# A fused attention and soft mixture-of-experts kernel: a list scheduler for the whole program, one pool of PSUM banks, and filler matmuls on TensorE

## The chip, the cores and the metric

One core of one Trainium2 chip runs the kernel. The metric is the device time of one execution in microseconds (us), lower is better. Executions of this kernel differ by some per cent: the kernel before gave 249 to 264 us. How long the chip grants TensorE its full clock differs from run to run (mean granted clock 0.68 to 0.79 before; the mean counts the time before the first recorded change as full). A run is called fast when it is within 1.5% of the fastest of its kernel, and slow otherwise. I quote medians of all runs, and the fast runs or their ratio where they say something else. Kernels ran beside runs of the kernel before.

## The reference

Eight batches of eight heads of windowed attention feed a soft mixture of experts. Cut to what matters:

```python
B, H, S, D = 8, 8, 576, 64                    # q, k, v: float32
scores = q @ k.T / 8                          # per batch and head
mask   = (rel >= 0) & (rel < 32)              # heads 0..3
       | (rel >= 0) & (rel < 128) & (rel % 4 == 0)   # heads 4..7
x = softmax(scores where mask) @ v            # -> (4608, 512)
logits = x @ phi                              # (4608, 32): 8 experts, 4 slots each
slot_in  = softmax(logits, over tokens).T @ x
slot_out = relu(slot_in[e] @ w1[e]) @ w2[e]   # w1 512x1024, w2 1024x512
out = softmax(logits, over slots) @ slot_out
```

## The kernel before

A batch is worked in two groups of four heads, so there are 16 groups g. In the loop TensorE does, for each group: `st_A` 72 staging transposes of q, k, v (four blocks of 18), `st_B` transposes of V, `st_S` scores (four blocks of 6), `st_P` probabilities times V (two blocks of 12), and for each batch `st_X` transposes of the result, `st_L` logits (8 dense matmuls of 288 columns), `st_E` and `st_I`, 48 narrow matmuls of 32 columns that accumulate into the PSUM bank `psA`. ScalarE evacuates st_A and does the exponentials; VectorE does the masks and the rest. The order of everything is written by hand, and PSUM banks come from two rings:

```python
ps2 = [... [128, 2, 512] ... for i in range(2)]     # two-bank tiles, two of them
ps1 = [... [128, 512] ...    for i in range(3)]     # one-bank tiles, three of them
psA = ...                                           # the accumulator
...
for step in range(-1, 2 * B + 2):
    if on: st_B(g, 0); st_S(g, 0, 0)
    if nx: st_A(g + 1, 0)
    if on: st_S(g, 0, 1)
    if nx: st_A(g + 1, 1)
    if pr: st_P(g - 1, 1)
    ...
    if odd: st_I(b - 1); st_X(b, 0); st_X(b, 1)
# loads, GpSimd queue: w1[0], q/k/v of batch 0 (whole), w1[1], q/k/v of batch 1, ...
```

After the loop come the two expert layers (`ffn1`, `ffn2`) and the output, 18 tiles.

The softmax here doesn't subtract the row's maximum and nothing guards it: scores larger than these inputs give would overflow.

## Time and profile before

| | before |
|---|---|
| median of the runs beside the change | 258.65 us (254.61 to 261.89, 4 runs) |
| profiled span | 261.6 us |
| first transposes start | 17.77 us |
| first expert matmul starts | 218.11 us |
| from there to the end | 43.5 us |

The page of the kernel before: span, busy time of TensorE (PE), VectorE (DVE), ScalarE (ACT), then in 40 slices of 6.5 us the busy tenths of TensorE, the granted clock in tenths, and the DMA engines' share.

```profile
span 261.6 us, 7056 instructions
PE 209.8 (80%) x3055; PEld 160.1 (61%) x3056; DVE 121.1 (46%) x237; ACT 125.2 (48%) x302; POOL 30.6 (12%) x68
PE   0027998999899989989998999899888758888700
PEclk9999999997557555555575575555555555999955
DMA  6999999999999509998910664178037700007998
```

TensorE is 90% busy or more through most of the loop, and the others aren't. The clock row reads half speed over most of it. Its first nine digits can't be taken at their word: the record holds changes of the clock, and reads full before the first one. The timeline of TensorE shows this (columns: start us, length us, engine, line, operation, tiles, shape, count).

```profile
27.03 0.93 PE L307 MATMUL ps_2<-ident,stg 96*64 96x96 bf16 x18
...
55.44 2.12 PE L417 MATMUL ps_0<-XT,phi_pad 128*128 128x288 bf16 x8
...
59.81 0.57 PE L307 MATMUL ps_2<-ident,stg 96*64 96x96 bf16 x18
60.31 0.73 PE L377 MATMUL ps_1<-VN,PT 128*96 128x65 bf16 x12
60.97 1.63 PE L457 MATMUL psA<-ET,XB 96*64 96x32 bf16 x48
62.53 0.66 PE L398 MATMUL ps_0<-ident,XB 96*128 96x96 bf16 x6
```

Eighteen staging transposes took 0.93 us at 27 us, where the clock row still says full, and 0.57 us at 59.81 us, so the loop was slow from its start. It got its full clock for one short stretch (58.4 to 61.8 us) after the dense logit matmuls of L417, and fell back. Four such stretches, 13.7 us, are all of the loop's 200.3 us: **7% at full clock**. That is the low end: this was a slow run, with a mean granted clock of 0.69, where the fast runs of this kernel had 0.75 to 0.79. No trace of those was kept. I work out this share the same way for every kernel below: stretches of full clock between the first transposes and the first expert matmul, leaving out the time before the first change where the transposes are slow.

The windows view of two batches (columns: busy us of PE, PEld, DVE, ACT and POOL with counts, granted clock, DMA share, GB/s), then the longest TensorE wait from the waits view:

```profile
84.40:109.20 24.80, 23.73 (x360) 19.48 (x358) 13.59 (x26) 14.87 (x38) 3.24 (x6) 0.53 0.66 129
109.20:132.60 23.40, 22.22 (x357) 18.18 (x357) 12.70 (x25) 12.91 (x34) 1.65 (x3) 0.55 0.95 191
...
PE ps_0 L307 <- DMA stg<-in_v_dram: 17.8, 1, 17.8
```

A batch takes 23.4 to 24.8 us, 95% of it TensorE busy at little more than half clock (0.53 and 0.55). Nothing waits long but the start.

### The profile page before, as it was taken

The page shows a single profiled execution, that of the slowest core. Times are in us where ns is not written, and L with a number is a line of the kernel's source. Part 1 is how long each engine was busy: PE and PEld are TensorE (multiplying, and loading weights), DVE is VectorE, ACT ScalarE, POOL GpSimd, SP SyncE. Part 2 cuts the span into 40 slices and gives each one's busy share as a digit, 9 for nine tenths or more (in the row PEclk, how much of TensorE's full clock was granted, in tenths as well). Part 3 has the DMA queues.
Part 4 walks back from the last instruction along what each step waited for, and adds up shares of the span by engine and source line. Part 5 has one row for each costly group of instructions (what it writes and reads, how often), then busy time and mean ns, then how long its engine had stood idle before and what let it go on. Part 6 is the DMA issues. An engine that isn't in the chain of part 4 may idle for free.

```text
span 261.6 us, 7056 instructions
## 1 busy us (share of the span) xinstructions
PE 209.8 (80%) x3055; PEld 160.1 (61%) x3056; DVE 121.1 (46%) x237; ACT 125.2 (48%) x302; POOL 30.6 (12%) x68
## 2 busy tenths in 40 slices
PE   0027998999899989989998999899888758888700
PEld 0025787778787867877787878778766734531100
DVE  0001557636644565466366545644664521219900
ACT  1017785565576545645655764456463010008900
POOL 7970300300030022002000000000000000000000
PEclk9999999997557555555575575555555555999955
DMA  6999999999999509998910664178037700007998
GB/s 110 207 219 208 220 209 217 214 215 212 219 198 216 118 4 189 220 219 153 215 37 3 114 113 99 19 148 147 18 38 137 152 0 3 3 0 289 406 404 345
DMA packets 8910, 40.88 MB, mean 156 GB/s; under 512 B 1456, under 2 KB 1456, under 8 KB 6832
## 3 DMA queue, kind: packets, MB, share of 16 engines
q0 software_dynamic: 5760, 30.94, 60.4%
q1 hardware_dynamic: 3120, 9.50, 9.2%
q8 instruction: 24, 0.39, 0.6%
q14 instruction: 6, 0.05, 0.0%
HBM read 61.93 MB, written 9.44 MB: 273 GB/s over the span
## 4 chain that ended last, share of the span: by engine, by line
PE 60%; ACT 10%; DMA 10%; DVE 9%; issue 4%; POOL 2%; POOLq 0%; ACTq 0%
DMA stg<-in_v_dram 10%; PE ps_1 L377 5%; PE psA L457 5%; PE ps_0 L377 4%; PE ps_2 L307 4%; PE ps_0 L307 4%; PE ps_1 L307 3%; PE ps_1 L587 3%; PE ps_0 L352 3%; PE ps_1 L417 3%; PE ps_0 L417 3%; DVE XB L386 3%; DVE w1r L612 3%; PE ps_1 L352 3%; ACT PT L358 3%
## 5 line engine op out<-in xcount | busy, mean ns | idle before, releaser
L307 PE MATMUL ps_0<-ident,stg 96*64 96x96 bf16 x414 | 21.2, 280 | 17.8 <-DMA stg<-in_v_dram 17.8
L358 ACT ACTIVATE PT<-ps_0 128x576 bf16<-128x576 f32 x32 | 21.1, 660 | 26.8 <-PE ps_0 L352 26.7
L358 ACT ACTIVATE PT<-ps_1 128x576 bf16<-128x576 f32 x32 | 21.1, 660 | 25.3 <-PE ps_1 L352 25.3
L361 DVE TENSOR_TENSOR PT<-PT,mask_d 128x576 bf16<-128x576 bf16 x32 | 14.7, 458 | 37.4 <-ACT PT L358 37.4
L307 PEld LDWEIGHTS ps_0<-ident,stg 96*64 96x64 bf16 x414 | 17.0, 162 | 20.7 <-POOL siT L293 17.7
L361 DVE TENSOR_TENSOR PT<-PT,mask_p 128x576 bf16<-128x576 bf16 x32 | 14.7, 458 | 25.8 <-ACT PT L358 25.1
L307 PE MATMUL ps_2<-ident,stg 96*64 96x96 bf16 x396 | 19.8, 275 | 0.2 <-DMA stg<-in_v_dram 0.2
L318 ACT ACTIVATE QT<-ps_0 128x288 bf16<-128x288 bf16 x23 | 10.4, 451 | 18.6 <-PE ps_0 L307 18.6
L377 PE MATMUL ps_1<-VN,PT 128*96 128x65 bf16 x192 | 17.8, 262 | 0.4 <-ACT PT L358 0.4
L377 PE MATMUL ps_0<-VN,PT 128*96 128x65 bf16 x192 | 17.8, 263 | 0.0
L307 PEld LDWEIGHTS ps_2<-ident,stg 96*64 96x64 bf16 x396 | 15.9, 159 | 3.1 <-issue 0.3
L377 PEld LDWEIGHTS ps_1<-VN,PT 128*96 128x96 bf16 x192 | 15.7, 183 | 2.3 <-PE ps_0 L352 0.6
L307 PE MATMUL ps_1<-ident,stg 96*64 96x96 bf16 x342 | 17.0, 274 | 0.0
L337 DVE COPY VN<-ps_1 128x768 bf16<-128x768 bf16 x12 | 6.6, 548 | 22.1 <-PE ps_1 L333 22.1
L377 PEld LDWEIGHTS ps_0<-VN,PT 128*96 128x96 bf16 x192 | 15.8, 184 | 1.6
L386 DVE TENSOR_TENSOR XB<-ps_0,RV 96x768 bf16<-96x768 f32 x16 | 15.3, 954 | 0.6
L386 DVE TENSOR_TENSOR XB<-ps_1,RV 96x768 bf16<-96x768 f32 x16 | 15.3, 953 | 0.6
L226 POOL DMA_DIRECT2D stg<-in_q_dram x8 | 4.4, 553 | 93.1 <-PE ps_1 L307 39.5
L307 PEld LDWEIGHTS ps_1<-ident,stg 96*64 96x64 bf16 x342 | 13.6, 158 | 2.4
L457 PE MATMUL psA<-ET,XB 96*64 96x32 bf16 x384 | 13.0, 217 | 0.6 <-DVE ET L443 0.6
L352 PE MATMUL ps_0<-QT,KT 64*128 64x96 bf16 x192 | 13.3, 267 | 0.0
L352 PE MATMUL ps_1<-QT,KT 64*128 64x96 bf16 x192 | 13.3, 267 | 0.0
(114 smaller groups left out, 377.8 us busy)
## 6 DMA issues: line engine op xcount, KB each, us to landing
out_dram<-w1r SPq DMA_DIRECT2D x18, 512.0 KB, 5.1
w1r<-in_moe_w_dram POOLq DMA_DIRECT2D x8, 1024.0 KB, 21.3
stg<-in_moe_w_dram POOLq DMA_DIRECT2D x6, 1024.0 KB, 8.0
stg<-in_q_dram POOLq DMA_DIRECT2D x8, 576.0 KB, 12.7
stg<-in_k_dram POOLq DMA_DIRECT2D x8, 576.0 KB, 14.8
stg<-in_v_dram POOLq DMA_DIRECT2D x8, 576.0 KB, 17.0
w2r<-in_moe_w_dram POOLq DMA_DIRECT2D x2, 1024.0 KB, 21.7
phi_st<-in_moe_phi_dram SPq DMA_DIRECT2D x1, 64.0 KB, 2.0
```

The source lines that it names most:

```text
L307: i_ = t.transpose(pbf[64 * hx:64 * hx + 64, NR * i:NR * i + NR], stg_x[s][0:NR, 2 * typ + hx, c, :], ident[0:NR, 0:NR])
L318: op("act", lambda ac, d=d, t=t: ac.activation(d, pv[:, t], ACTF.Copy), r=[pb], **{"w" if r == 0 else "a": [bd[par]]})
L337: op("dve", lambda vv: vv.tensor_copy(vt[:, half, :, :, 0:64], pbf[:, 0:768].rearrange("p (m x d) -> p m x d", m=NB, x=2)), r=[pb], w=[vb[ ...
L352: i_ = t.matmul(sc[:, hx, QB * mm:QB * mm + QB], KT[par][64 * hx:64 * hx + 64, half, QB * m:QB * m + 128], QT[par][64 * hx:64 * hx + 64, h ...
L358: op("act", lambda ac: ac.activation(pt[:], sc[:, :, 0:3 * QB], ACTF.Exp, scale=SCALE), r=[scb], w=[ptb])
L361: op("dve", lambda vv: vv.tensor_tensor(pt[:], pt[:], mk.unsqueeze(1).to_broadcast([128, 2, 3 * QB]), AluOp.mult), r=[b_mask[typ]], w=[ptb])
L377: i_ = t.matmul(po[0:QB, hx, 65 * m:65 * m + 65], pts[m // 3][0][:, hx, QB * (m % 3):QB * (m % 3) + QB], vt[:, half, m, hx, 0:65], start=T ...
L386: op("dve", lambda vv: vv.tensor_tensor(xd, pv[:, :, :, 0:64], rv[:].unsqueeze(3).to_broadcast([QB, 2, NB, 64]), AluOp.mult), r=[pob, rvb] ...
L417: i_ = t.matmul(lg[:, hf, 0:288], phi_pad[:, c].rearrange("p j i -> p (j i)"), XT[:, c, 288 * hf:288 * hf + 288], start=c == 0, stop=c == 3)
L457: i_ = t.matmul(psA[64 * typ:64 * typ + 64, 32 * c:32 * c + 32], x_, et[:, NB * typ + m, :], start=(b == 0 and m == 0 and c == 0), stop=(b ...
L587: i_ = t.matmul(sp_[32 * j:32 * j + 32, :], hT[:, hi, cc, j, :], w2v[e][:, cc, :], start=(hi == 0 and cc == 0), stop=(hi == 1 and cc == 7))
L612: op("dve", lambda vv, o=o, po=po: vv.tensor_scalar(ost[:, o % NO, 1, :], po[:, 1, :], rtok[:, 2 * o + 1:2 * o + 2], None, op0=AluOp.mult) ...
```

## The change

Its intent: let a program order the work so that TensorE never waits, and keep its clock up where it still does.

1. Work is first collected as tasks with estimated durations (taken at full clock) and due times, then placed by a list scheduler, which also picks PSUM banks from one pool of seven. The outcome is a fixed order for each engine; nothing is decided on the chip.
2. Where the plan leaves TensorE idle for 0.27 us or more, up to six unused 384-column matmuls go into spare columns of `psA` (84 in all).
3. q, k, v are loaded in halves per group, ahead of w1, and the set-up memsets moved from GpSimd to VectorE.

```diff
-    for step in range(-1, 2 * B + 2):      # hand-written order
+def place(tasks, banks, filler):
+    ...                                    # per engine: earliest start, given preds, banks
+            if e == "pe" and t.mode != last_mode[0]:
+                st += 0.13
+            m = min(c[0] for c in cands)
+            st, t = min((c for c in cands if c[0] <= m + 0.14), key=lambda c: (c[1].due, c[1].idx))
+    ...
+        if t.eng == "pe":
+            idle = st - free.get("pe", 0.0)
+            if filler is not None and order:
+                f = filler(idle, st)
...
-    ps2 = [A(nc.psum_tensor(f"ps2_{i}", [128, 2, 512], F32)) for i in range(2)]
-    ps1 = [A(nc.psum_tensor(f"ps1_{i}", [128, 512], F32)) for i in range(3)]
+    NBK = 7
+    psum = A(nc.psum_tensor("psum", [128, NBK, 512], F32))
...
-    def load_qkv(b):                       # whole batch; w1[0] before batch 0
+    def load_qkv(b, due):
+        for typ in range(2):
+            for t, src in enumerate((q, k, v)):
+                load(...)                  # half a batch each; w1[0] after batch 0
...
+    def filler(idle, st):
+        n_ = min(int((idle - 0.1) / 0.17), 6)
+        if n_ < 1 or acc_last[0].end is not None:
+            return None
+        ...
+                i_ = pe.matmul(psA[:, 128:512], ident[:, :],
+                               mask[1][:, 0:4, :].rearrange("p m x -> p (m x)"),
+                               start=False, stop=False, skip_group_check=True)
```

## The prediction

> **What bounds the kernel now.** From 17.8 us (first landing of q, k, v; before it TensorE waits 17.8 us, the longest TensorE wait) to about 209 us TensorE is 91 to 98% busy in nearly every 10 us stretch (windows view); VectorE and ScalarE are busy 45 to 65%. The chain of waits is 60% TensorE. One batch (two head groups) takes 23.75 us: the accumulation into psA starts at 61.0, 84.4, 109.2, 132.7, 156.1, 180.9, 203.5. So TensorE bounds the main loop, and it runs slowly: 18 staging transposes take 0.93 us nearly everywhere but 0.57 us in 58 to 61 and 82 to 86 us; 12 probability-times-V matmuls take 1.17 against 0.73 us. The granted clock reads 0.50 over most of 60 to 218 us. Before 57 us it reads 1.0, but the durations there are the slow ones, so I take the clock to be half there too. The fast stretches follow the eight dense 288-column logit matmuls. The Trainium skill ("TensorE: Matmul & The Clock Gate", Part 1) says the clock is halved until TensorE was busy for one window of about 3.4 us, and Part 4 that transposes don't count as busy in the same way. The trace agrees: fast stretches last about 4 us, and over half of the loop's matmuls are transposes.
>
> Loads aren't the bound: 31 MB at 215 GB/s is 144 us, and the DMA queues idle from 130 us on for want of staging buffers.
>
> **What changes.**
> 1. First landing: q, k, v come in halves and first, ahead of w1. 0.88 MB at 215 GB/s is 4 us plus issue and latency: TensorE starts near 9 us. Saves about 8 us, all on the chain.
> 2. Order: waits inside the loop are only 5% of TensorE's time; this and one bank pool give at most 1 us per batch at half clock. The end (205 to 218 us, one long dependence chain) may lose 2 us.
> 3. Filler matmuls, 384 columns each, about 0.16 us fast and 0.32 us at half clock. Alone they are cost, and TensorE has no slack at half clock. Their worth is the clock. From the fast stretches, a group needs about 6.5 us of TensorE work plus some 1.7 us of switching and waits, so about 8.2 us against 11.9 us; ScalarE needs about 6.5 and VectorE about 6 (start to start), loads 6.8 per group, so nothing else binds much earlier.
> 4. Unchanged: experts and output, 43 us from 218 us; output DMA at 405 GB/s.
>
> Always fast: 9 + 16 x 8.2 + 5 + 7 + 43 = 195 us. Always slow with fillers: 9 + 16 x 12 + 10 + 43 = 254 us. The planner places fillers only where its own (fast) plan leaves TensorE idle by 0.27 us, so they may be too thin to hold the clock everywhere. I expect fast for about three quarters of the loop: 210 us.
>
> **Predicted: 210 us, 80% between 193 and 242. Faster by over 2%: 0.93; within 2%: 0.05; slower: 0.02.**
>
> **What would show it.** Step 1: first transposes near 9 us. Step 3: granted clock near 1.0 over most of 15 to 145 us, 18 transposes near 0.57 us, batch period 16 to 18 us; TensorE busy share falls or holds while ScalarE and VectorE shares rise. Step 2: TensorE waits spread, few over 1 us. Step 4: last 43 us alike.
>
> **What would make it wrong.** The fillers are too few: clock remains 0.5, period 23 us or more, time near 250. Or the clock holds but ScalarE or the loads become the bound, with periods of 19 us. Or the last w2 tiles, whose buffers come free only after batch 7's transposes, land after the first expert layer ends.

## The result, and the profile after

The changed kernel took 209.73 us (median of 4 runs, 207.09 to 212.37), against 258.65 us. The ratio of the fast runs is 0.815, 95% interval 0.8035 to 0.8264. A ratio is the mean time of one kernel's fast runs over that of the other's of the same rounds, so it is not quite the ratio of the medians. The profiled run of the changed kernel took 211.77 us (span 210.0 us), one of its slower ones. That of before took 263.31 us, more than the four runs in the table, so the two profiles compare slow with slow.

The page of the changed kernel, the rows shown of before:

```profile
span 210.0 us, 7124 instructions
PE 169.3 (81%) x3139; PEld 125.0 (60%) x3140; DVE 119.8 (57%) x259; ACT 122.8 (58%) x302; POOL 36.1 (17%) x71
PE   0479998968999995999889998999989888798000
PEclk9999999999967998599999999557999669999955
DMA  5999999999999999999999999962990000069998
```

TensorE's busy share is nearly the same, 81% after 80%, of a shorter span: its 40 us less are the same work at a higher clock, and 84 matmuls more. The clock row is now mostly full, and here the early digits hold. The timeline of TensorE:

```profile
16.22 0.57 PE L448 MATMUL psum<-ident,stg 96*64 96x96 bf16 x18
...
128.23 0.78 PE L622 MATMUL psA<-ET,XB 96*64 96x32 bf16 x20
129.63 1.03 PE L622 MATMUL psA<-ET,XB 96*64 96x32 bf16 x28 [0.62 <-issue]
130.59 0.66 PE L553 MATMUL psum<-ident,XB 96*128 96x96 bf16 x6
131.19 0.42 PE L498 MATMUL psum<-QT,KT 64*128 64x96 bf16 x6
131.54 0.82 PE L472 MATMUL psum<-ident,VT 128*128 128x128 bf16 x6
132.29 0.93 PE L448 MATMUL psum<-ident,stg 96*64 96x96 bf16 x18
```

The clock is full from 11.1 us. It falls three times within the loop, for 6.8, 6.8 and 13.7 us; the last fall is the one above, and the transposes are back at 0.93 us. At the loop's end it falls once more. Full clock for **81% of the loop**.

Where the 51.6 us between the two profiled spans come from:

| part | before | after | gain |
|---|---|---|---|
| start to first transposes | 17.77 | 10.0 | 7.8 |
| loop, to first expert matmul | 200.3 | 156.1 | 44.2 |
| experts and output | 43.5 | 43.9 | -0.4 |

The windows view of two batches, and the two longest TensorE waits (waits view):

```profile
96.00:113.00 17.00, 15.26 (x355) 12.47 (x352) 11.93 (x25) 13.25 (x36) 1.13 (x2) 1.00 1.03 214
113.00:128.20 15.20, 14.49 (x327) 11.76 (x324) 11.80 (x25) 11.59 (x29) 1.06 (x2) 1.00 1.05 217
...
PE psA L787 <- DVE mask_d L415: 8.0, 1, 8.0
PE psum L448 <- issue: 4.3, 3, 2.1
```

These two take 17.0 and 15.2 us at full clock; the first took 19.6 us, at full clock as well. The 8.0 us are the first fillers waiting for their operand at the start, before any data is there, and "issue" is idle time for which the profile shows no cause. So the clock is the visible difference. The open question is what holds it: the fillers (theory A, the prediction's), or the planned order (theory B).

### The profile page after: what moved, and what is told of

Its sections match the earlier page's. It is cut to its first block, busy times and chain, and to the rows that moved or that the text cites. A ratio compares the mean times of both kernels' runs of the same rounds, so it can differ in the third digit from the quotient of the medians.

```text
span 210.0 us, 7124 instructions
## 1 busy us (share of the span) xinstructions
PE 169.3 (81%) x3139; PEld 125.0 (60%) x3140; DVE 119.8 (57%) x259; ACT 122.8 (58%) x302; POOL 36.1 (17%) x71
## 4 chain that ended last, share of the span: by engine, by line
PE 58%; DVE 15%; ACT 12%; issue 7%; DVEq 0%
PE psum L448 10%; PE psum L526 8%; PE psum L498 6%; PE psA L622 6%; PE psum L472 6%; DVE w1r L765 5%; PE psum L553 5%; PE psA L787 4%; PE psum L737 4%; PE psum L682 3%; PE psum L576 3%; ACT QT L458 3%; ACT PT L504 3%; ACT KT L458 2%; DVE XB L538 2%
## 5 line engine op out<-in xcount | busy, mean ns | idle before, releaser
L504 ACT ACTIVATE PT<-psum 128x576 bf16<-128x576 f32 x64 | 42.3, 668 | 28.1 <-PE psum L498 27.5
L448 PE MATMUL psum<-ident,stg 96*64 96x96 bf16 x1152 | 36.1, 225 | 4.3 <-issue 4.3
L458 ACT ACTIVATE QT<-psum 128x288 bf16<-128x288 bf16 x64 | 30.0, 468 | 12.1 <-PE psum L448 12.1
L448 PEld LDWEIGHTS psum<-ident,stg 96*64 96x64 bf16 x1152 | 31.3, 123 | 8.6 <-issue 6.5
L538 DVE TENSOR_TENSOR XB<-psum,RV 96x768 bf16<-96x768 f32 x32 | 30.5, 954 | 1.1
L458 ACT ACTIVATE VT<-psum 128x288 bf16<-128x288 bf16 x64 | 30.5, 478 | 0.4 <-PE psum L448 0.4
L458 ACT ACTIVATE KT<-psum 128x288 bf16<-128x288 bf16 x64 | 30.4, 476 | 0.0
L476 DVE COPY VN<-psum 128x768 bf16<-128x768 bf16 x32 | 17.6, 552 | 17.9 <-PE psum L472 17.9
L526 PE MATMUL psum<-VN,PT 128*96 128x65 bf16 x384 | 24.7, 217 | 2.2 <-DVE PT L507 0.8
L787 PE MATMUL psA<-mask_d,ident 128*128 128x384 bf16 x84 | 19.6, 348 | 8.0 <-DVE mask_d L415 8.0
L526 PEld LDWEIGHTS psum<-VN,PT 128*96 128x96 bf16 x384 | 21.8, 132 | 5.4 <-DVE PT L507 2.7
L498 PE MATMUL psum<-QT,KT 64*128 64x96 bf16 x384 | 20.7, 216 | 3.9 <-issue 1.5
L472 PE MATMUL psum<-ident,VT 128*128 128x128 bf16 x192 | 18.1, 237 | 0.0
```

The lines of the kernel that those rows point to most:

```text
L448: i_ = t.transpose(o[64 * hx:64 * hx + 64, NR * i:NR * i + NR], stg_x[s][0:NR, 2 * typ + hx, c, :], ident[0:NR, 0:NR])
L458: op("act", lambda ac, d=d, t=t: ac.activation(d, bf(h)[:, 0:9 * NR].rearrange("x (c t h p) -> x t h p c", c=9, t=3, h=2)[:, t], ACTF.Copy ...
L472: i_ = t.transpose(o[:, 128 * m:128 * m + 128], VT[par][:, half, QB * m:QB * m + 128], ident[:, :])
L476: op("dve", lambda vv: vv.tensor_copy(vt[:, half, :, :, 0:64], bf(h)[:, 0:768].rearrange("p (m x d) -> p m x d", m=NB, x=2)), w=[vb], ps=[ ...
L498: i_ = t.matmul(sc[:, hx, QB * mm:QB * mm + QB], KT[par][64 * hx:64 * hx + 64, half, QB * m:QB * m + 128], QT[par][64 * hx:64 * hx + 64, h ...
L504: op("act", lambda ac: ac.activation(pt[:], f32(h)[:, :, 0:3 * QB], ACTF.Exp, scale=SCALE), w=[ptb], ps=[h], dur=0.54, due=due + 0.2)
```

## The experiments

All results are correct against the reference. Times are medians, with lowest and highest.

### 1. The change without its fillers

```diff
-    for t in place(tasks, NBK, filler):
+    for t in place(tasks, NBK, None):
```

> The changed kernel with its 84 filler matmuls left out; planned order, one bank pool and loads untouched. Theory A (the fillers hold the clock, and the clock is the gain): the granted clock falls to 0.5 over most of the loop, 18 staging transposes go back to 0.93 us, time 235 to 252 us. Theory B (the planned order alone packs TensorE densely enough to hold the clock; the fillers are a cost): 200 to 210 us with the clock unchanged. In between (220 to 232): both take part.

Measured: 212.39 us (210.32 to 218.0, 4 runs), before beside it 261.14 us. The page's rows, then the windows view of one long stretch at full clock and of two batches:

```profile
PE   0279999997889899699897999987946788898000
PEclk9999999999999999859999559999955579999855
...
36.50:87.70 51.20, 44.20 (x1082) 36.99 (x1077) 36.22 (x74) 40.87 (x107) 12.84 (x24) 1.00 1.05 215
61.50:77.10 15.60, 14.14 (x341) 11.81 (x338) 12.10 (x25) 12.43 (x33) 4.32 (x9) 1.00 1.05 214
97.90:113.40 15.50, 13.51 (x345) 11.65 (x344) 11.50 (x25) 13.02 (x36) 1.13 (x2) 1.00 1.02 213
```

Theory A falls. Without any filler the loop still runs at full clock for 63% of the time, from 36.5 us on, and the kernel takes some 3 us more than the changed kernel's 209.5 us. That was on another chip; as a share of the kernel before beside each, the medians are alike (0.813 here, 0.811 and 0.817 for the changed kernel), so even these 3 us aren't sure.

The two batches of 15.5 us flatter the order. A batch is 356 matmuls of the loop's own (2848 in all, for eight), and in the planned order the time from one accumulation to the next holds more or less than that: 341 and 345 in these two, and 396 in the first, which took 18.8 us at full clock. By count, the stretch of 51.2 us makes 16.8 us a batch, and all three stretches of full clock within the loop (99.0 us, 2091 matmuls) 16.9 us. The count is a rough measure, as matmuls differ in length.

### 2 and 3. Fillers in the old order

One, and then two, of the same fillers after each of the 64 score blocks of the kernel before (psA set to zero first, as the change does):

```diff
             st_S(g, 0, 0)
+            fill(1)          # experiment 3: fill(2); likewise after the other three
```

> The kernel before, in its old order with its old banks and loads, with one 384-column filler matmul after each of the 64 score blocks. Theory A (clock is the gain): if 64 regular fillers are enough to hold the clock, about 225 us (loop period from 23.7 to about 19.5 us, start unchanged); if they are too thin they only cost 64 x 0.32 us at half clock, up to 270 us. Theory B (the order is the gain): 260 to 270 us.

> As e2 with two fillers after each score block, 128 in all. Theory A: the clock holds, 225 to 232 us, in spite of 128 more matmuls. Theory B: 270 to 285 us, the fillers being pure cost.

Measured: 247.59 us (246.85 to 258.15) with 64 fillers and 244.38 us (240.01 to 257.25) with 128, against 261.14 us. The fast runs were 246.85 to 247.59 us and 240.01 to 242.23 us, against 251.36 us, the one fast run of before; so the gain of the 64 is small. The page's clock row of the second, and a batch of it:

```profile
PEclk9999999999555799999997999999999657999955
...
106.20:126.70 20.50, 18.18 (x374) 13.28 (x372) 12.70 (x25) 13.85 (x36) 1.65 (x3) 1.00 1.04 215
```

Full clock for 55% and 76% of the loop. So dense fillers do raise the clock, and the old order gets quicker in spite of up to 128 more matmuls: neither "pure cost" nor the predicted 225 us. But 76% of full clock is close to the change's 81%, and the kernel is 35 us slower. Eight of these are the start; 128 fillers at 0.16 us are 20 us more, by estimate from the changed kernel, where six fast ones span 1.15 us with the last one's own 0.34 us ((1.15 - 0.34) / 5). The 7 us left are about what the gaps of the old order would cost (experiment 8). The old order has to buy its clock with work.

### 4 and 8. The start, from both sides

The changed kernel with w1[0] first and batch 0 waiting for both halves:

```diff
+    load_w1(0, -27.0)
     for b in range(B):
         load_qkv(b, -26.0 + b)
...
-        op("pe", pe, r=[b_id, b_in[s][typ]], ...
+        op("pe", pe, r=[b_id, b_in[s][typ]] + ([b_in[s][1]] if b == 0 else []), ...
```

> The changed kernel, but the first w1 tile is loaded ahead of q, k, v again and batch 0 waits for both its halves, so the first transposes start near 17 us instead of 10. If TensorE's own work paces the loop the 7 us come back in full: about 214 to 217 us. If something later in the loop (loads, ScalarE) sets the pace, less than 3 us: 208 to 211 us.

Measured: 216.64 us (210.71 to 218.23), first transposes at 17.84 us, loop 156.1 us as in the changed kernel. By the medians that is the seven microseconds in full, but the control ran on another chip, the profiled spans differ by 5.2 us (210.0 and 215.2, the part after the loop being 2.6 us shorter), and the one fast run, 210.71 us, is only 1.5 to 4.6 us above the control's. The loop itself took up none of the late start.

The kernel before with q, k, v in halves and ahead of w1:

```diff
-    load_w1(0)
...
     load_qkv(0)               # now two halves, each group waits for its own
-    load_w1(1)
+    load_w1(0)
```

> The kernel before with q, k, v loaded in halves per head group and ahead of w1, and nothing else of the change. If the start is worth what it moves: first transposes near 10 us, 6 to 8 us faster than before, 250 to 254 us, clock as before. If the earlier data also let TensorE hold its clock in the loop: 240 us or less. If the loop swallows it: 258 us or more.

Measured: 247.94 us (243.73 to 253.71, 6 runs) against 256.51 us; ratio of fast runs 0.9762, interval 0.9566 to 0.9959. First transposes at 9.57 us. The medians gain 8.6 us, a little above the range; the fast runs gain 6 us (2.4%), within it. So the gain is the start's. In the profiled run, a fast one, the clock was full for 27% of the loop, which gives what was missing, the old order at full clock with no fillers, in one stretch and in the batch within it:

```profile
48.20:72.10 23.90, 19.81 (x483) 16.64 (x482) 15.07 (x31) 17.74 (x46) 5.31 (x10) 1.00 1.05 213
52.20:70.40 18.20, 14.74 (x357) 12.33 (x356) 12.47 (x25) 13.38 (x36) 3.70 (x7) 1.00 1.05 213
```

By count of matmuls, all four stretches of full clock in this loop (51.2 us, 1007 matmuls) make 18.1 us a batch, against 16.9 us in the planned order of experiment 1: at the same clock, the order is worth about 1.2 us a batch. TensorE is busy 80% of the time in the first (40.90 of 51.20) and 87% in the second (86.46 of 99.00). So the planned order closes some of the gaps that the full clock opens; in the batch shown TensorE waited 2.1 us for VectorE (`XB`) and 1.2 us for ScalarE (`VT`). Loads don't pace this stretch: q, k and v of the groups begun in it had landed 9 us before or more.

### 5 and 6. The change again, and fillers at the start only

Run 5 is the changed kernel unchanged, the control. Run 6 keeps the fillers of the plan's first 36 us, 22 of 84:

```diff
-        if n_ < 1 or acc_last[0].end is not None:
+        if n_ < 1 or st > 36.0:
```

> The changed kernel once more, unchanged, as the control for the runs beside it: 206 to 213 us, granted clock near 0.9, fast from about 11 us on.

> The changed kernel with fillers only in the first 36 us of the plan (22 of the 84). New theory C (the order gains the time; the fillers win only the first stretch, which stayed slow to 36 us without them, and later they cost 0.16 us each): fast from about 11 us, and 2 to 6 us faster than the control, 203 to 208 us. Theory A (fillers hold the clock all along): the clock falls for most of the time after 40 us, 220 us or more.

Measured: 209.49 us (206.15 to 211.26) for the control, ratio 0.826 to before; 208.46 us (204.56 to 211.39) for run 6. No difference beyond the spread, so 62 of the 84 fillers may go or stay. The expected gain of 2 to 6 us did not show: the medians differ by 1.0 us, and the one fast run of run 6, 204.56 us, is 1.6 us below the control's fastest. In its profiled run, a slow one, the clock was full for 70% of the loop. It also shows a long stretch in the new order at half clock:

```profile
75.50:96.00 20.50, 20.44 (x324) 17.67 (x320) 10.25 (x21) 13.55 (x36) 3.19 (x6) 0.50 1.04 214
98.10:113.70 15.60, 13.54 (x347) 11.62 (x346) 11.67 (x25) 13.04 (x36) 1.13 (x2) 1.00 1.03 214
```

At half clock TensorE is busy 20.44 of 20.50 us. From one accumulation to the next (74.5 to 98.1 us, with 3 us of it at full clock) it took 23.6 us, nearly as in the kernel before (23.4), though with 388 matmuls in place of 357: by count 21.7 us a batch. At half clock TensorE has almost no gaps for an order to close (95% busy before); the 1.7 us gained by count come from one stretch.

### 7. The old split of the banks under the new scheduler

```diff
-        for b0 in range(banks - h.n + 1):
+        for b0 in ((0, 2) if h.n == 2 else (4, 5, 6)):
```

> The changed kernel, but its planner may place two-bank tiles only in banks 0-1 and 2-3 and one-bank tiles only in banks 4, 5, 6, as the kernel before had them. If the one pool is what frees the order: batch period back towards 20 us and 225 us or more. If banks were not what held the old order up: within 3 us of the control.

Measured: 212.95 us (206.38 to 214.75) against 209.49 us for the control; full clock for 63% of the loop in a slow profiled run. The one fast run, 206.38 us, equals the control's (206.15 and 206.4). At most a few microseconds, and the spreads overlap: the one pool is not what made the change.

### 9, 10 and 11. What kind of work holds the clock

The old order, with 768 moving columns of extra TensorE work at the head of each score block, written to spare columns of that block's bank, in three kinds:

```diff
         def pe(t):
+            for x_ in range(4):                     # 9: full-array matmuls, 192 columns
+                t.matmul(sc[:, 0, 288:480], ident[:, :], mask columns, ...)
+            for x_ in range(6):                     # 10: transposes, 128 columns
+                t.transpose(sc[:, 0, 288:512] as bf16, 128 of its columns, ident, ident)
+            for x_ in range(4):                     # 11: a 32 x 32 corner, 192 columns
+                t.matmul(sc[0:32, 0, 288:480], ident[0:32, 0:32], mask[0:32] columns, ...)
             for mm in range(3):
```

> The kernel before, old order, with 768 moving columns of unused full-array matmuls (4 of 192 columns) at the head of each of the 64 score blocks. Close to e3 (two 384-column fillers after each block): the clock fast over about three quarters of the loop, 240 to 250 us. Control for the two runs beside it.

> As e9, with the same 768 columns streamed by six 128-column transposes instead of matmuls. If the clock answers to any TensorE work, as in e9: 240 to 250 us. If transposes don't count (as the prediction took from the Trainium skill): the clock stays at half over nearly the whole loop and each block costs 0.64 us more, 285 to 305 us.

> As e9, with the same 768 columns streamed through a 32 x 32 corner of the array. If the clock counts the time that matmuls stream, as in e9: 240 to 250 us. If it counts how much of the array works: the clock stays at half, 285 to 305 us.

| kind | median us (range) | before beside it | full clock in the loop |
|---|---|---|---|
| 9 matmuls | 245.82 (242.91 to 248.6) | 256.12 | 77% |
| 10 transposes | 248.96 (244.23 to 249.88) | 256.12 | 73% |
| 11 corner | 277.64 (274.94 to 281.0) | 256.12 | 34% |

The windows view of the whole loop of 9, 10 and 11, then the clock row of 11:

```profile
18.10:200.90 182.80, 157.38 (x3108) 127.03 (x3112) 102.71 (x204) 110.17 (x280) 15.40 (x28) 0.91 0.78 155
```

```profile
17.90:203.70 185.80, 160.66 (x3236) 133.86 (x3238) 102.81 (x204) 110.43 (x280) 15.67 (x28) 0.90 0.77 153
```

```profile
17.90:231.40 213.50, 198.10 (x3104) 154.25 (x3104) 104.48 (x204) 113.55 (x280) 15.63 (x28) 0.78 0.68 133
PEclk9999999999985995755579759957975555799965
```

Transposes hold the clock as matmuls do; my assumption that they don't falls. The corner of the array holds it far less: its TensorE is busy 93% of the loop (198.10 of 213.50), more than the 86% of run 9, and it gets 34%. So "busy" in the profile isn't what the clock answers to; how much of the array works matters. Whether the corner counts at all isn't shown: 34% is above the 7% of the kernel before, but that was its slow run, and the mean granted clock of run 11 (0.80) is about that of the fast runs of before beside it (0.75 to 0.79).

### 12. Fillers inside the narrow accumulation

In several runs the clock fell just behind the 48 narrow matmuls of st_I. So: early and late fillers as planned, and between them five fillers inside each accumulation but the last.

```diff
             for m in range(3 * k_, 3 * k_ + 3):
+                if m < 5 and b < B - 1:
+                    t.matmul(psA[:, 128:512], ...)     # the filler
                 i_ = pe(t, m)
...
-        if n_ < 1 or acc_last[0].end is not None:
+        if n_ < 1 or acc_last[0].end is not None or 36.0 < st < 138.0:
```

> The changed kernel with early fillers and those of the last stretch, and in place of the ones between five fillers inside each 48-matmul accumulation into psA, behind which the clock fell in most runs so far. If these stretches are where the clock is lost: fast over 90% of the loop, 200 to 206 us in spite of 35 fillers (about 6 us). If the clock falls elsewhere as well: 208 to 214 us.

Measured: 222.82 us (212.08 to 232.74), full clock for 56% of the loop in a slow profiled run. It failed: five of its six runs were slow, and the one fast run, 212.08 us, is still above the changed kernel's fast ones (206.15 to 209.26). The timeline of TensorE around one fall at 76.3 us:

```profile
75.79 0.34 PE L632 MATMUL psA<-mask_d,ident 128*128 128x384 bf16 x1
76.05 0.42 PE L622 MATMUL psA<-ET,XB 96*64 96x32 bf16 x8
76.41 0.50 PE L632 MATMUL psA<-mask_d,ident 128*128 128x384 bf16 x1
76.84 0.68 PE L622 MATMUL psA<-ET,XB 96*64 96x32 bf16 x16
```

The filler takes 0.34 us, and the next one 0.50: the clock fell amid the fillers. It then remained at half until 96.8 us, with TensorE busy without a gap. Where a few dense matmuls stand decides little alone; why this arrangement did so much worse than the plan's own isn't settled.

## Why the prediction was right or wrong, point by point

- **The total, 210 us: right** (209.73 and, again, 209.49 us). So was its split: 8 us at the start, nearly all the rest in the loop, the tail alike. In part it is luck: the total rests on a guess that the clock would be full for three quarters of the loop, held there by the fillers. The share came out near that (81%), but beyond the first stretch the fillers weren't what held it.
- **What bounds the kernel: right.** TensorE at half clock, with the early part of the clock row set aside for the durations.
- **Step 1, start near 9 us, 8 us saved: right.** 10.0 us; 7.8 us between the profiles, 6 us by the fast runs (8.6 by the medians) alone on the kernel before, 7 us by the medians the other way round.
- **Step 2, "this and one bank pool give at most 1 us per batch at half clock": the step that failed.** As a sum of waits it isn't far off: at full clock the order is worth about 1.2 us a batch by itself, 18.1 against 16.9. What the step left out is that the order moves the clock. With the planned order and without a single filler the loop had its full clock for 63% of the time, where the old order with early loads had 27% (both profiled runs were fast ones), and the loop took 157.1 us against 191.2: 34 us, or over 4 us a batch. For the one pool alone, a few us at most was right.
- **Step 3, "Their worth is the clock": wrong about who holds it.** The clock was indeed full for "about three quarters of the loop" (81%). But leaving all fillers out cost about 3 us, if that, and leaving out 62 of 84 cost nothing measurable. They win the first stretch (full from 11.1 us, and from 16.7 us in the control, in place of 36.5 us), but the loop took 157.1 us without them, and with them 156.1 us in the slow profiled run and 153.1 us in the fast one (the control): most of what they win they take up again as work. In the old order it took fillers to raise the clock.
- **"Transposes don't count": wrong**, by runs 9 and 10. I took it from the Trainium skill, "TensorE: Matmul & The Clock Gate", Part 4, and read the trace as agreeing. That the loop was slow while over half of its matmuls were transposes is so, but their kind wasn't the reason.
- **Signs:** batch period 16 to 18 us: 15 to 17.6 us in the later batches where the clock was full, 19.6 us in the first, mean 18.0. TensorE waits few over 1 us: held, but for the start and stalls of up to 2.1 us where the profile shows nothing that TensorE waits for.

How much of the loop's 44 us is the clock, by estimate: the old order took about 25 us a batch at half clock (the three batches that start at 84.4, 109.2 and 156.0 us with their short fast stretches taken out) and 18.2 us at full. Its loop of 13.7 us fast and 186.6 us slow is then 8.2 batches of work, and they would take 158 us at 81% full clock, as in the changed kernel (156.1), and 166 us at 63%, as in experiment 1 (157.1). For experiment 8, at 27%, the estimate gives 187 us where 191.2 were measured, so it is good to about 5 us. By it, some 34 us of the 43 us that the loop gained without fillers passes through the clock, and the rest is the order's own; in the changed kernel the fillers' work takes up about as much as the order itself gains. That the planned order holds the clock *because* it packs TensorE more densely is argued, from the busy shares at full clock (80 against 87%) and from runs 9 to 11, where density of array work alone moved the clock. No run changed the density of the planned order alone, so it is not shown. That it is the order at all is shown by exclusion: without fillers (run 1), without the one pool (run 7) and with the late load (run 4) the loop kept its 156 to 161 us, but each was left out by itself, never all together. The falls of the clock that remain, 27 us of half clock in the loop, and the stalls without a visible cause are left open.

## What to carry to other kernels

Read the clock from the durations of one repeated instruction, not from the clock row alone, and cost each part of a change at the clock that the changed kernel will have: an order that saves little by its waits may be what keeps the clock full. When fillers are added to hold the clock, run the kernel without them before crediting them. And a TensorE that is 95% busy, as before the change, can still be short of clock; with matmuls in a corner of the array (run 11) it was 93% busy and had 34%.

## What the Trainium skill lacked or had wrong

- "TensorE: Matmul & The Clock Gate", Part 4 (PE-mode transpose), says that the full clock doesn't engage for transposes, which don't count as TensorE activity in the same way. Here the same 768 columns per block held the full clock for 73% of the loop as transposes and for 77% as matmuls (248.96 and 245.82 us), and 18 transposes ran in 0.57 us at full clock, in place of 0.93 us.
- The same page, Part 1, speaks of TensorE being busy or idle over a window, and its closing table warns of idle gaps of over about 3 us. It doesn't say that the amount of the array in use counts: with 32 x 32 matmuls TensorE was 93% busy and had full clock for 34% of the loop, with full-array matmuls 86% busy and 77%. And the clock stayed at half for 20.5 us with TensorE busy for 20.44 of them. How much of the array has to work it doesn't say; these runs don't show it either.
- Its window of about 3.4 us agrees: stretches between changes of the clock were 3.4, 6.8 and 13.7 us.
- The same page's warning that clock events can be unreliable lacks the case met here, and no page I read has it: before the first recorded change the profile shows full clock, while 18 transposes at 27.03 us took 0.93 us, the half-clock time.
